# One side bank for the long TensorE tiles, and a new list of VectorE's exp groups, in a fused attention and MLP kernel

## The chip, the core and the metric

The kernel runs on one core of a Trainium2 chip. The metric is the device time of one execution in microseconds, as the median over runs. The profile comes from one execution that the hardware profiler recorded. Its engines are TensorE (PE, with its weight loads as PEld), VectorE (DVE), ScalarE (ACT), GpSimd (POOL) and SyncE (SP), which issues most of the DMAs.

## The reference

The sequence has 2048 rows of 448 columns, in bf16. There are 16 heads of 28 columns, and the inner width of the MLP is 1792.

```python
xn = _layernorm(x, axis=-1)
s = _A_ref(xn, A_wqkv, A_wo)          # attention: softmax(q k^T * 28**-0.5) v, then @ wo
g = _silu(_B_ref(xn, B_w1, B_b1, B_w2, B_b2))   # gelu(xn @ w1 + b1) @ w2 + b2, then silu
return x + s * g
```

## The kernel before

**Blocks and tiles.** The heads are put in four groups `g` of four heads, the rows in four chunks `c` of 512. A block is one pair (g, c), so there are 16 of them, run in the order of `b = 4 g + c`. A block has 64 score tiles of 128 x 512: 16 key tiles `t` for each of four heads `j`. In all there are MTOT = 1024 tiles, numbered by `m`. The last block is cut into three parts of 256, 128 and 128 query columns, so that the end comes in small steps. A score matmul (L1223) uses 32 rows of TensorE's array, and those of different heads run side by side. P*V (L1494) adds 32-column matmuls into one PSUM bank, `acc`; four of them run side by side.

**The banks.** PSUM has eight banks: six of `ring`, and `acc` and `misc`. Units of score tiles alternate between ring banks 0 to 2 (three tiles) and 4 to 5 (two tiles). ScalarE's exp (L1279) reads a whole unit at once and writes bf16 tiles into free places of `P`, `h` or `xnT`. `acc` belongs to P*V once it has begun. Two side banks are left, `misc` and ring bank 3, for everything else: the projections of Q and K (`p_q`, `p_k`, L744), of V (`p_v0`, `p_v1`, L1031), the first MLP matrix (`p_f1`, L1089), the second (`p_f2`, L1158), the output projection (`p_out`, L1591), the sums and reciprocals at a block's end (`p_epi`), and score tiles for VectorE.

**VectorE's groups.** `QUADS` lists groups of four consecutive tiles, `4 q` to `4 q + 3`, whose exp VectorE computes. For each tile a score matmul goes into a side bank (`p_late`), either joined to a unit's score task or by itself, and VectorE evicts it with a scale and an offset into 16-bit integers (`p_apass`, L1382). Five VectorE instructions over 2048 columns (`p_expq`, L1433 to L1440) then make the three summands of the exp, which P*V reads as three tiles in place of one. Each group needs three places of 2048 columns until P*V has read them.

**The order of the work.** The order of instructions is made while the kernel is built. Every piece of work is a Python generator; it yields tasks for an engine, or asks for a bank under a condition. A planner (`run`) keeps an estimated time for each engine and each buffer, and always puts the task that can start first. Among tasks of one engine that can start within EPS = 0.1 us of each other, it goes by priority (scores before most others) and then by the order in which the pieces of work were spawned. The engines then run their fixed lists, each strictly in order, with semaphores between them. The condition with which a projection asks for a bank before the change is this:

```python
bank, tok = yield ("bank", lambda: K.ready(K.b_xnT[c] + [K.b_wqk[1][g]]) and (g == 0 or K.boot()))
```

The bank goes to the piece of work as soon as the inputs are ready and a bank is free, and comes back after VectorE has evicted it. For `p_f2` seven tasks of two matmuls each lie between the two. Fillers (`p_busy`, L905) add zeros to `acc` where the planner sees TensorE too little in use for its clock.

**Stages.** The start (layer norm, transposes, projections of group 0) takes some 20 us. Then the stream of exps runs to the end, with the other work between. Before block 9 is over ScalarE runs the whole GELU at once (L1138), partly from ring banks. F2 and silu's tanh (L1173) follow, then the output projections. Chunks 0 to 2 of the output are added into DRAM by DMAs on GpSimd's queue (L1608), where the input was copied before; the last chunk is added on VectorE and stored by SP. `late_on` is set when the layer norm and the transposes are done, and lets VectorE's groups begin.

Of the kernel before, what the change touches and what calls it, by code (L numbers as in the profile page):

```python
# [18 lines left out]
G = 4  # L19
C = 4  # L20
# [7 lines left out]
MTOT = NBLK * T * 4  # L28

GM = 64 * 9 + 6  # L30
QUADS = (17, 22, 25, 36, 37, 59, 65, 72, 82, 87, 99, 103, 115, 122, 129, 135, 138, 142, 152, 153, 157, 158, 164, 168, 178, 180, 194, 199, 211, 213, 222, 229, 234, 242)
SM_SCALE = DH ** -0.5
LOG2E = 1.4426950408889634
EXP_A3, EXP_A2, EXP_LC = 0.16391228, 0.00783292, 1.1187538523466403
# [5 lines left out]
ND = 9  # L40
# [36 lines left out]
class _Kernel:  # L77
# [132 lines left out]
    def run(self):  # L210
        idle = 0
        while True:
# [25 lines left out]
            self.put(p[3], s)  # L238
            self.advance(p)

    def ready(self, toks, ahead=0.0):
        return all(b.tw is not None and b.tw <= self.now + ahead for b in toks)

# [143 lines left out]
    def schedule(self):  # L387
        K = self
        K.n_f1 = 0
        K.exp_u = -1  # L390
        K.exp_m = -1
        K.late_ready = []
        K.sc_u = -1
        K.pv_m = -1
        K.E_done = -1
        K.norms_done = False
        K.stg_done = 0
        K.qsqs = [0, 1]
        K.qn = [[] for _ in range(G)]
        K.qn_done = 0  # L400
        K.q0_done = 0
        K.f2n = [0] * C
        K.pv_started = False
        K.chunks_done = 0
        K.g_done = [False] * C
        K.on_done = [False] * NBLK
        K.on4 = [False] * 4
        K.ln_done = 0
        K.taken = 0
        K.next_m = 0  # L410
        K.n_late = 0
        K.gu = None
        K.pend = None
        K.units = []
        K.pv_done = [False] * MTOT
        K.late = {4 * q + k for q in QUADS for k in range(4)}
        K.late_left = [sum(1 for q in QUADS if K.sub_of(4 * q) == b) for b in range(NBLK + 3)]
        K.late_on = False
        K.PB, K.PPREV, K.plast = {}, {}, {}
        K.free_u = []  # L420
        K.a_left = {}
        K.ln2e = 0
        K.late_blk = 0
        K.banks += [(K.ring[:, b, :], K.b_ring[b]) for b in (3, 2)]
        K.outs = []
        K.gelu_done = False
        K.dir_n = 0
        K.dir_read = 0
        self.constants()
        self.loads()  # L430
        for c in range(C):
            K.spawn(K.p_ln(c), c)
        K.spawn(K.p_first(), 0)
        K.spawn(K.p_scores(), 0)
        K.spawn(K.p_take(2), 0)
        K.spawn(K.p_exps(), 0)
        K.spawn(K.p_pv(), 0)
        K.spawn(K.p_units(), 0)
        K.spawn(K.p_late(), 0)
        K.spawn(K.p_busy(), 100)  # L440
        o = 1.0

        def nxt():
            nonlocal o
            o += 1.0
            return o
        K.spawn(K.p_norms(), nxt())
        for c in range(1, C):
            K.spawn(K.p_tr(c, 0), nxt())
            K.spawn(K.p_tr(c, 1), nxt())  # L450
            K.spawn(K.p_k(0, c), nxt())
            if c == 1:
                K.spawn(K.p_v0(0), nxt())
            K.spawn(K.p_v0(c), nxt())
        K.spawn(K.p_q(0, 1), nxt())
        for c in (2, 3):
            K.spawn(K.p_q(0, c), nxt())
        for c in range(C):
            K.spawn(K.p_k(1, c), nxt())
        K.spawn(K.p_q(1, 0), nxt())  # L460
        for t in range(T):
            K.spawn(K.p_v1(t), nxt())
        for c in (1, 2, 3):
            K.spawn(K.p_q(1, c), nxt())
        K.spawn(K.p_qn(1), nxt())
        f1 = deque(SBT)
        for c in range(C):
            for _ in range(4):
                K.spawn(K.p_f1(*f1.popleft()), nxt())
            K.spawn(K.p_k(2, c), nxt())  # L470
            K.spawn(K.p_q(2, c), nxt())
        K.spawn(K.p_qn(2), nxt())
        while f1:
            K.spawn(K.p_f1(*f1.popleft()), nxt())
        for c in range(C):
            K.spawn(K.p_k(3, c), nxt())
            K.spawn(K.p_q(3, c), nxt())
        K.spawn(K.p_qn(3), nxt())
        K.spawn(K.p_gelu(), 0)
        K.spawn(K.p_direct(), 0)  # L480
        for c in range(C):
            for t in range(4):
                K.spawn(K.p_f2(c, t), nxt())
            K.spawn(K.p_silu(c), nxt())
        K.o_epi = 0.5
        for c in range(C - 1):
            for t in range(4):
                K.spawn(K.p_out(c, t), nxt())
        for t in range(4):
            K.spawn(K.p_last(t), nxt())  # L490
        K.run()
        for h in K.outs:
            K.wait(SP, h)
# [473 lines left out]

    def p_k(self, g, c):
        K = self
        bank, tok = yield ("bank", lambda: K.ready(K.b_xnT[c] + [K.b_wqk[1][g]]) and (g == 0 or K.boot()))  # L970
        for k in range(2):
            yield K.t_proj(1, g, c, bank, tok, k, 1.5 if g == 0 else 5)
        yield K.t_kev(DVE, g, c, bank, tok, 1 if g == 0 else 2)
        K.banks.append((bank, tok))

    def p_q(self, g, c):
        K = self
        bank, tok = yield ("bank", lambda: K.ready(K.b_xnT[c] + [K.b_wqk[0][g], K.b_colK, K.b_kT[0][3]]) and ((g, c) == (0, 1) or K.boot()))
        for k in range(2):
            yield K.t_proj(0, g, c, bank, tok, k, 1.5 if g == 0 else 5)  # L980
        qb = K.qT[:, g, c * 512:(c + 1) * 512]
        qr = _Buf()
        yield _Task(DVE, lambda eng: eng.tensor_copy(qb, bank), [tok], [qr], 0.7, 0.0, 2)
        K.banks.append((bank, tok))
        yield ("until", lambda: len(K.qsqs) > 0 if g == 0 else (K.qn_done >= g - 1 and (g > 1 or K.q0_done == 3)))
        i = K.qsqs.pop(0) if g == 0 else c
        qs, tq = K.qsq[:, i, :], K.b_qsq[i]
        yield _Task(DVE, lambda eng: eng.tensor_tensor(qs, qb, qb, ALU.mult), [qr], [tq], 0.43, 0.0, 2)
        if g:
            K.qn[g].append(qr)  # L990
            return
        bank2, tok2 = yield ("bank", lambda: K.ready([tq]))
        yield _Task(PE, lambda eng: eng.matmul(bank2, K.bsel[:, :], qs, start=True, stop=True),
                    [tq, K.b_bsel], [tok2], 0.216, 0.17, 1.5 if g == 0 else 4)
        K.qsqs.append(i)
        yield _Task(DVE, lambda eng: eng.scalar_tensor_tensor(qb, bank2, K.colK[:, g:g + 1], qb, op0=ALU.add,
                                                              op1=ALU.add), [tok2, K.b_colK, qr], [qr, K.b_qT[g][c]], 0.75, 0.0, 2)
        K.banks.append((bank2, tok2))
        K.q0_done += 1
# [56 lines left out]
    def p_v1(self, t):  # L1056
        K = self
        rd = [K.b_wv, K.b_wvpad] + K.b_xnT[t // 4]
        bank, tok = yield ("bank", lambda: K.ready(rd + [K.b_vpad]) and K.boot())
        yield _Task(PE, K.t_v([t], 4, 16, bank, tok), rd, [tok], 0.65, 0.17)  # L1060
        yield K.t_vev([t], 4, 16, bank, tok)
        K.banks.append((bank, tok))

    def p_f1(self, c, ft):
        K = self
        bank, tok = yield ("bank", lambda: K.ready(K.b_xnT[c] + [K.b_w1, K.b_w1pad]) and K.stg_done == 2 and K.norms_done)
        for k in range(2):
            yield K.t_f1(c, ft, bank, tok, k)
        wr = [K.b_hf[c][ft]]
        K.hf_free(c, ft)  # L1070
        dst = K.h[:, c, ft * 512:(ft + 1) * 512]
        yield _Task(DVE, lambda eng: eng.tensor_copy(dst, bank), [tok], wr, 0.69, 0.0, 2)
        K.banks.append((bank, tok))
        K.n_f1 += 1
# [73 lines left out]

    def p_f2(self, c, t):
        K = self  # L1150
        bank, tok = yield ("bank", lambda: K.b_h[c].tw is not None and K.ready([K.b_h[c], K.b_w2]) and K.dir_read == ND and (c < 2 or K.g_done[c - 2]))
        hv = K.h[:, c, :].rearrange("p (f n) -> p f n", n=512)
        ps = bank[:, 0:D]
        for q in range(7):
            def f(eng, q=q):
# [3 lines left out]
                                     start=(ft == 0), stop=(ft == FT - 1))  # L1159
                return ins  # L1160
            yield _Task(PE, f, [K.b_w2, K.b_h[c]], [tok], 0.378, 0.17)
        fb = K.fsb[:, c % 2, t, :]
        yield _Task(DVE, lambda eng: eng.tensor_tensor(fb, ps, K.b2b[:, :], ALU.add), [tok, K.b_b2], [K.b_fsb[c % 2]],
                    0.63, 0.0, 2)
# [446 lines left out]
    
    def p_out(self, c, t):
        K = self
        bank, tok = yield ("bank", lambda: K.on_done[(G - 1) * C + c] and K.g_done[c])
        ps = bank[:, 0:D]
        yield K.t_wo(ps, tok, c, t, (0, 1))
        yield K.t_wo(ps, tok, c, t, (2, 3))
        yield from K.t_oev(ps, tok, c, t)
        K.banks.append((bank, tok))

# [62 lines left out]
```

## Time and profile before

| What | us |
|---|---|
| median of 5 runs | 461.03 |
| lowest and highest | 460.93, 461.48 |
| the profiled execution's own time | 460.93 |
| its span, first to last instruction | 459.1 |

In a row of the page's group table, the line, the engine, the operation and the tiles come first, then how many there were, the busy time and the mean duration in ns, then the engine's idle time just before them and what ended it. A row of the waits reads: who waited, for whom, the total in us, how often, and the longest. A row of the timeline begins with the start and the length in us. Durations of neighbours on one engine can overlap, so the time from one start to the next is often shorter than a duration. The row of PEclk gives TensorE's granted clock in tenths, over 40 equal slices of the span.

### The profile page before, as it was taken

What the parts mean: (1) busy time and instruction counts of PE and PEld (TensorE: products, weight loads), DVE (VectorE), ACT (ScalarE), POOL (GpSimd) and SP (SyncE); (2) the same over time, 40 slices, a digit from 0 to 9 for tenths busy, and PEclk for the clock granted to TensorE, in tenths of its full rate; (3) what the DMA queues carried; (4) which work ended last, traced back from release to release, by engine and by line L of the source; (5) the groups of instructions that cost most, each with busy time, mean ns of one, the idle gap of its engine ahead of it and who ended that gap; (6) DMA issues with size and microseconds to landing.
All of it is one profiled execution on the core that took longest, in us unless ns stands there. A gap on an engine that the chain in (4) does not pass through costs nothing.

```text
span 459.1 us, 10615 instructions
## 1 busy us (share of the span) xinstructions
PE 436.2 (95%) x4431; PEld 161.8 (35%) x4431; DVE 372.9 (81%) x584; ACT 446.8 (97%) x408; POOL 41.0 (9%) x85
## 2 busy tenths in 40 slices
PE   6999999999999999999999999999999999989994
PEld 5533333333332323323233333333323333343452
DVE  8956898894897797978989989847778978999964
ACT  6999999999999999999999999999999999999994
POOL 7470000000000000000000000000000100101111
PEclk9999999999999999999999999999999999999998
DMA  8701000000000000000040000000000001300331
GB/s 263 274 2 37 2 1 0 1 1 4 1 1 0 1 2 3 1 2 1 0 143 1 2 0 2 1 1 0 1 1 2 1 0 43 42 1 1 42 43 41
DMA packets 8049, 11.16 MB, mean 24 GB/s; under 512 B 1697, under 2 KB 6993, under 8 KB 7954
## 3 DMA queue, kind: packets, MB, share of 16 engines
q1 hardware_dynamic: 6850, 8.43, 5.9%
q0 software_dynamic: 864, 1.38, 2.5%
q8 instruction: 35, 0.57, 0.5%
q10 hardware_dynamic: 288, 0.69, 0.4%
q14 instruction: 12, 0.10, 0.1%
HBM read 8.61 MB, written 3.21 MB: 26 GB/s over the span
## 4 chain that ended last, share of the span: by engine, by line
PE 42%; ACT 41%; issue 12%; DVE 3%; DMA 1%; POOL 0%; ACTq 0%; DVEq 0%; POOLq 0%
ACT P L1279 20%; PE ring L1223 12%; ACT xnT L1279 10%; ACT h L1279 8%; PE acc L1494 7%; PE ring L1089 5%; PE acc L905 3%; PE misc L1158 2%; PE misc L744 2%; PE misc L1089 2%; PE ring L1158 2%; PE ring L744 2%; PE misc L1223 1%; ACT w L1173 1%; PE ring L1031 1%
## 5 line engine op out<-in xcount | busy, mean ns | idle before, releaser
L1279 ACT ACTIVATE P<-ring 128x1024 bf16<-128x1024 f32 (+1 forms) x188 | 217.5, 1263 | 1.4 <-PE ring L1223 1.0
L1223 PE MATMUL ring<-qT,kT 32*128 32x512 bf16 (+2 forms) x1074 | 145.1, 358 | 11.4 <-ACT P L1279 5.6
L1279 ACT ACTIVATE h<-ring 128x1024 bf16<-128x1024 f32 (+1 forms) x102 | 117.7, 1264 | 0.2
L1223 PEld LDWEIGHTS ring<-qT,kT 32*128 32x128 bf16 x1074 | 37.6, 91 | 134.1 <-ACT P L1279 55.3
L1279 ACT ACTIVATE xnT<-ring 128x1536 bf16<-128x1536 f32 (+1 forms) x72 | 83.4, 1306 | 0.0
L1494 PE MATMUL acc<-P,vaug 128*32 128x512 bf16 (+2 forms) x524 | 49.2, 358 | 0.0
L1089 PE MATMUL ring<-xnT,w 128*128 128x512 bf16 x156 | 41.4, 382 | 1.1 <-ACT h L1138 0.9
L1564 POOL CAST rhi<-rc 128x16 bf16<-128x16 f32 x15 | 6.0, 401 | 365.2 <-DVE rc L1562 297.0
L905 PE MATMUL acc<-ident,zero 128*128 128x128 bf16 x393 | 34.3, 221 | 0.0
L1223 PE MATMUL misc<-qT,kT 32*128 32x512 bf16 (+1 forms) x78 | 29.2, 376 | 0.0
L905 PEld LDWEIGHTS acc<-ident,zero 128*128 128x128 bf16 x393 | 22.3, 98 | 18.8 <-issue 18.2
L1494 PE MATMUL acc<-h,vaug 128*32 128x512 bf16 x248 | 27.6, 384 | 0.0
L1158 PE MATMUL misc<-w,h 128*128 128x448 bf16 x112 | 27.3, 356 | 0.0
L1158 PE MATMUL ring<-w,h 128*128 128x448 bf16 x112 | 27.2, 355 | 0.0
L1382 DVE TENSOR_SCALAR x_sb<-misc 128x512 uint16<-128x512 f32 x31 | 21.3, 687 | 6.2 <-PE misc L1223 5.9
L1089 PE MATMUL misc<-xnT,w 128*128 128x512 bf16 x68 | 19.5, 383 | 0.5 <-DVE qT L1581 0.5
L1552 DVE CAST E_sb<-acc 128x512 bf16<-128x512 f32 x15 | 10.4, 690 | 11.7 <-PE acc L1494 11.7
L1494 PE MATMUL acc<-xnT,vaug 128*32 128x512 bf16 (+2 forms) x240 | 18.7, 330 | 0.9 <-ACT P L1279 0.7
L1089 PEld LDWEIGHTS ring<-xnT,w 128*128 128x128 bf16 x156 | 12.1, 97 | 20.0 <-issue 7.2
L1494 PEld LDWEIGHTS acc<-P,vaug 128*32 128x32 bf16 x524 | 11.8, 94 | 15.0 <-issue 11.8
L1382 DVE TENSOR_SCALAR kT<-ring 128x512 uint16<-128x512 f32 x19 | 13.1, 688 | 4.3 <-PE ring L1223 3.4
L1138 ACT ACTIVATE h<-h 128x2048 bf16<-128x2048 bf16 (+2 forms) x8 | 16.2, 2031 | 0.0
(269 smaller groups left out, 662.5 us busy)
## 6 DMA issues: line engine op xcount, KB each, us to landing
w<-in_B_w_dram SPq DMA_DIRECT2D x1, 1568.0 KB, 7.7
w<-in_B_w_dram SPq DMA_DIRECT2D x1, 1344.0 KB, 8.5
out_dram<-in_A_x_dram SPq DMA_DIRECT2D x3, 448.0 KB, 11.3
out_dram<-h POOLq DMA_DIRECT2D x6, 224.0 KB, 3.9
x_sb<-in_A_x_dram SPq DMA_DIRECT2D x2, 448.0 KB, 5.7
h<-in_A_wqkv_dram SPq DMA_DIRECT2D x3, 168.0 KB, 5.1
x_sb<-in_A_x_dram ACTq DMA_DIRECT2D x1, 448.0 KB, 4.5
h<-in_A_x_dram SPq DMA_DIRECT2D x1, 448.0 KB, 4.2
```

The costliest lines, as they stand in the source:

```text
L744: ins = eng.matmul(bank, w[:, kt, g * 128:(g + 1) * 128], K.xnT[:, kt, c * 512:(c + 1) * 512], start=(kt == 0), stop=(kt == KT - 1))
L905: ins = eng.matmul(K.acc[:, 0:128], K.zero[:, :], K.ident[:, :], start=False, stop=True, skip_group_check=True)
L1031: ins = eng.matmul(bank[:, off:off + nh * 32], K.xnT[:, kt, t * 128:(t + 1) * 128], ap, start=(kt == 0), stop=(kt == KT - 1), skip_group_c ...
L1089: ins = eng.matmul(bank, K.w1[:, kt, ft * 128:(ft + 1) * 128], K.xnT[:, kt, c * 512:(c + 1) * 512], start=(kt == 0), stop=(kt == KT - 1))
L1138: yield _Task(ACT, lambda eng, dst=dst, src=src: eng.activation(dst, src, ACTF.Gelu_apprx_tanh), rd, wr, 0.4267 * n + (0.1 if pc else 0.06 ...
L1158: ins = eng.matmul(ps, hv[:, ft, t * 128:(t + 1) * 128], K.w2[:, ft, :], start=(ft == 0), stop=(ft == FT - 1))
L1223: return eng.matmul(dst, K.kT[32 * j:32 * j + 32, g, t * 128:(t + 1) * 128], K.qT[32 * j:32 * j + 32, g, c * 512 + q0:c * 512 + q0 + nq], ...
L1279: return eng.activation(reg[:, i0:i0 + n, :], K.ring[:, b0:b0 + n, :], ACTF.Exp, scale=SM_SCALE)
L1382: yield _Task(DVE, lambda eng: eng.tensor_scalar(K.unit[u][:, 512 * k:512 * k + 512].bitcast(dt.uint16), bank, SM_SCALE * LOG2E * 128.0, ( ...
L1494: return eng.matmul(K.acc[32 * j:32 * j + 32, q0:q0 + nq], K.vaug[:, t, 4 * g + j, :], ap[:, col:col + nq], tile_position=(0, 32 * j), sta ...
L1552: yield _Task(DVE, lambda eng: eng.tensor_copy(E, K.acc[:, :]), [K.b_acc], [tE], 0.7, 0.0, 0)
L1564: yield _Task(POOL, lambda eng: eng.tensor_copy(K.rhi[:, :], K.rc[:, :]), [K.b_rc], [K.b_rhl], 1.1, 0.0, 1)
```

## The change

There are two edits. The list `QUADS` goes from 34 groups to 35, and only ten groups stand in both lists. By block, the eleventh (counted from one) goes from two groups to three, the fourteenth from three to two and the fifteenth from two to three; the other blocks keep their number, with most groups in other places. The second edit counts the pieces of work that hold a side bank and still have matmuls to issue. While the count is not zero, no other piece of these kinds gets a bank: `p_k`, `p_q`, `p_v1`, `p_f1`, `p_f2` and `p_out`. The count goes down after the last matmul is put, before VectorE's eviction. Before `late_on` the gate is open.

```diff
-QUADS = (17, 22, 25, 36, 37, 59, 65, 72, 82, 87, 99, 103, 115, 122, 129, 135, 138, 142, 152, 153, 157, 158, 164, 168, 178, 180, 194, 199, 211, 213, 222, 229, 234, 242)
+QUADS = (17, 18, 25, 37, 41, 58, 68, 70, 81, 90, 97, 98, 117, 124, 131, 135, 140, 142, 146, 154, 157, 159, 161, 162, 165, 183, 185, 197, 200, 210, 211, 225, 229, 234, 242)
...
+    def pe_free(self):
+        return self.pe_wait == 0 or not self.late_on
...
+        K.pe_wait = 0
...
     def p_f2(self, c, t):
         K = self
-        bank, tok = yield ("bank", lambda: K.b_h[c].tw is not None and K.ready([K.b_h[c], K.b_w2]) and K.dir_read == ND and (c < 2 or K.g_done[c - 2]))
+        bank, tok = yield ("bank", lambda: K.pe_free() and K.b_h[c].tw is not None and K.ready([K.b_h[c], K.b_w2]) and K.dir_read == ND and (c < 2 or K.g_done[c - 2]))
+        K.pe_wait += 1
...
             yield _Task(PE, f, [K.b_w2, K.b_h[c]], [tok], 0.378, 0.17)
+        K.pe_wait -= 1
...
     def p_out(self, c, t):
         K = self
-        bank, tok = yield ("bank", lambda: K.on_done[(G - 1) * C + c] and K.g_done[c])
+        bank, tok = yield ("bank", lambda: K.pe_free() and K.on_done[(G - 1) * C + c] and K.g_done[c])
+        K.pe_wait += 1
         ps = bank[:, 0:D]
         yield K.t_wo(ps, tok, c, t, (0, 1))
         yield K.t_wo(ps, tok, c, t, (2, 3))
+        K.pe_wait -= 1
```

`p_k`, `p_q`, `p_v1` and `p_f1` get the same three lines around their matmuls.

More of the change, by code (lines that the diff above doesn't have):

```diff
@@ L969, in p_k @@
         K = self
-        bank, tok = yield ("bank", lambda: K.ready(K.b_xnT[c] + [K.b_wqk[1][g]]) and (g == 0 or K.boot()))
+        bank, tok = yield ("bank", lambda: K.pe_free() and K.ready(K.b_xnT[c] + [K.b_wqk[1][g]]) and (g == 0 or K.boot()))
+        K.pe_wait += 1
         for k in range(2):
             yield K.t_proj(1, g, c, bank, tok, k, 1.5 if g == 0 else 5)
+        K.pe_wait -= 1
         yield K.t_kev(DVE, g, c, bank, tok, 1 if g == 0 else 2)
@@ L977, in p_q @@
         K = self
-        bank, tok = yield ("bank", lambda: K.ready(K.b_xnT[c] + [K.b_wqk[0][g], K.b_colK, K.b_kT[0][3]]) and ((g, c) == (0, 1) or K.boot()))
+        bank, tok = yield ("bank", lambda: K.pe_free() and K.ready(K.b_xnT[c] + [K.b_wqk[0][g], K.b_colK, K.b_kT[0][3]]) and ((g, c) == (0, 1) or K.boot()))
+        K.pe_wait += 1
         for k in range(2):
             yield K.t_proj(0, g, c, bank, tok, k, 1.5 if g == 0 else 5)
+        K.pe_wait -= 1
         qb = K.qT[:, g, c * 512:(c + 1) * 512]
@@ L1058, in p_v1 @@
         rd = [K.b_wv, K.b_wvpad] + K.b_xnT[t // 4]
-        bank, tok = yield ("bank", lambda: K.ready(rd + [K.b_vpad]) and K.boot())
+        bank, tok = yield ("bank", lambda: K.pe_free() and K.ready(rd + [K.b_vpad]) and K.boot())
+        K.pe_wait += 1
         yield _Task(PE, K.t_v([t], 4, 16, bank, tok), rd, [tok], 0.65, 0.17)
+        K.pe_wait -= 1
         yield K.t_vev([t], 4, 16, bank, tok)
@@ L1065, in p_f1 @@
         K = self
-        bank, tok = yield ("bank", lambda: K.ready(K.b_xnT[c] + [K.b_w1, K.b_w1pad]) and K.stg_done == 2 and K.norms_done)
+        bank, tok = yield ("bank", lambda: K.pe_free() and K.ready(K.b_xnT[c] + [K.b_w1, K.b_w1pad]) and K.stg_done == 2 and K.norms_done)
+        K.pe_wait += 1
         for k in range(2):
             yield K.t_f1(c, ft, bank, tok, k)
+        K.pe_wait -= 1
         wr = [K.b_hf[c][ft]]
@@ L1150, in p_f2 @@
         K = self
-        bank, tok = yield ("bank", lambda: K.b_h[c].tw is not None and K.ready([K.b_h[c], K.b_w2]) and K.dir_read == ND and (c < 2 or K.g_done[c - 2]))
+        bank, tok = yield ("bank", lambda: K.pe_free() and K.b_h[c].tw is not None and K.ready([K.b_h[c], K.b_w2]) and K.dir_read == ND and (c < 2 or K.g_done[c - 2]))
+        K.pe_wait += 1
         hv = K.h[:, c, :].rearrange("p (f n) -> p f n", n=512)
@@ L1161, in p_f2 @@
             yield _Task(PE, f, [K.b_w2, K.b_h[c]], [tok], 0.378, 0.17)
+        K.pe_wait -= 1
         fb = K.fsb[:, c % 2, t, :]
@@ L1613, in p_out @@
         K = self
-        bank, tok = yield ("bank", lambda: K.on_done[(G - 1) * C + c] and K.g_done[c])
+        bank, tok = yield ("bank", lambda: K.pe_free() and K.on_done[(G - 1) * C + c] and K.g_done[c])
+        K.pe_wait += 1
         ps = bank[:, 0:D]
@@ L1617, in p_out @@
         yield K.t_wo(ps, tok, c, t, (2, 3))
+        K.pe_wait -= 1
         yield from K.t_oev(ps, tok, c, t)
```

## The prediction

> **What bounds the kernel now.** I read the page first (busy shares and the clock row), then the waits by engine, then the groups by form, then ScalarE's timeline, and last the timeline of the end.
>
> ```profile
> PE 436.2 (95%) x4431; PEld 161.8 (35%) x4431; DVE 372.9 (81%) x584; ACT 446.8 (97%) x408; POOL 41.0 (9%) x85
> ...
> PEclk9999999999999999999999999999999999999998
> ```
>
> TensorE (PE) and ScalarE (ACT) both look full, so the shares alone do not tell which one leads. The waits do.
>
> ```profile
> PEld ring L1223 <- ACT P L1279: 55.3, 135, 0.8
> PEld ring L1223 <- ACT h L1279: 33.2, 78, 0.6
> ...
> PEld ring L1223 <- ACT xnT L1279: 19.5, 49, 0.7
> ```
>
> ```profile
> ACT P L674 <- DMA x_sb<-in_A_x_dram: 2.3, 1, 2.3
> ACT P L1279 <- PE ring L1223: 1.0, 3, 0.5
> ```
>
> The score matmuls (L1223) wait 108 us in 262 places for ScalarE's exp (L1279) to give a bank back; ScalarE's recorded waits for scores are 1.0 us. Also 393 of TensorE's matmuls, 34.3 us of busy time, are fillers (L905) without work in them. So ScalarE leads, and a time for the change is a time for ScalarE: how many exps it runs, and how often one starts late. The exps by form:
>
> ```profile
> L1279 ACT ACTIVATE P<-ring 128x1536 bf16<-128x1536 f32 x85 | 127.6, 1501 | 0.5 <-PE ring L1223 0.2
> L1279 ACT ACTIVATE P<-ring 128x1024 bf16<-128x1024 f32 x102 | 106.5, 1070 | 0.9 <-PE ring L1223 0.8
> L1279 ACT ACTIVATE h<-ring 128x1536 bf16<-128x1536 f32 x44 | 66.4, 1508 | 0.2
> L1279 ACT ACTIVATE h<-ring 128x1024 bf16<-128x1024 f32 x58 | 61.7, 1079 | 0.0
> L1279 ACT ACTIVATE xnT<-ring 128x1536 bf16<-128x1536 f32 x36 | 54.6, 1515 | 0.0
> L1279 ACT ACTIVATE xnT<-ring 128x1024 bf16<-128x1024 f32 x36 | 39.5, 1096 | 0.0
> ...
> L1279 ACT ACTIVATE P<-ring 128x512 bf16<-128x512 f32 x1 | 0.6, 639 | 0.0
> ```
>
> There are 165 exps over three tiles, 196 over two and one over a single tile: 888 tiles. Their durations overlap, so the price of one is its pitch, from start to start:
>
> ```profile
> 306.27 1.16 ACT L1279 ACTIVATE P<-ring 128x1024 bf16<-128x1024 f32 x1
> 307.17 7.03 ACT L1279 ACTIVATE xnT<-ring 128x1536 bf16<-128x1536 f32 x6
> ```
>
> An exp of two tiles is followed after 0.90 us. Over all starts in the trace the common pitch is 0.904 us for two tiles, 1.330 us for three and 0.478 us for the single one. At these pitches the stream costs 196 x 0.904 + 165 x 1.330 + 0.478 = 397.1 us. The real starts add 8.3 us to that, 6.7 us of it in 41 exps that start more than 0.06 us late. The page hides these, because a late start first eats the overlap of the durations (1.070 - 0.904 = 0.17 us) before it shows as idle time. In most of the 41 TensorE ran a projection, F1 or F2 task, or a P*V task, when the bank came back.
>
> **The change, part by part.**
>
> The list: 35 groups of four tiles leave ScalarE where 34 did, so 884 tiles stay. In the changed instruction order there are 164 three-tile and 196 two-tile exps, and no single one: 196 x 0.904 + 164 x 1.330 = 395.3 us. ScalarE saves 1.330 + 0.478 = 1.81 us. It is on the path at full value, since ScalarE's stream is almost without a pause from the first exp at 13.94 us to the last at 451.82 us.
>
> VectorE (DVE) takes the group: four evictions (L1382) at 0.69 us and the five steps of its exp (L1433 to L1440): three of 0.69 us and two of 1.22 us. That is 2.75 + 4.5 = 7.3 us, and nine instructions. VectorE is idle for 459.1 - 372.9 = 86 us; its share goes from 81% to 83%. Where the time lies matters more. Counting instructions in program order by the durations of their rows, the 15 exps that follow the 230th had 9.9 us of VectorE work beside 18.6 us of ScalarE, and get 17.0 us. Other stretches of 15 exps already stand at 0.95 to 1.04 in the present order, and in the new one the fullest (exps 110 to 125) stands at 1.05. I cost it at nothing; the cover is VectorE's idle time within each block, and if it is gone the rival below holds.
>
> TensorE: scores stay at 960 matmuls. A VectorE tile needs three P*V matmuls in place of one: 4 x 2 = 8 more, and 8 of them take 0.45 us, four running side by side. The fillers go from 393 to 429, 36 x 0.056 = 2.0 us, put where TensorE would pause. Both lie in TensorE's waits for ScalarE (108 us). Cost: nothing by themselves.
>
> The gate (`pe_free`, `pe_wait`): while one projection, V, F1, F2 or output tile has matmuls left, no second one may take a side bank. Such tiles finish one after the other in the present order too, so no matmul is lost by this; what it changes is that the second bank stays free for score tiles of VectorE's groups. VectorE waits for those scores now, for example
>
> ```profile
> DVE x_sb L1382 <- PE misc L1223: 5.9, 11, 1.8
> ...
> DVE kT L1382 <- PE ring L1223: 3.4, 7, 1.0
> ```
>
> This gives VectorE room rather than time. The price is that F2 tiles finish some exps later: the last one's eviction stands behind exp 304 where it stood behind 297, and the tanh over its chunk moves with it. The output projections of the last chunk but one move from before VectorE's copy of the last block's first half to after it. Both are far from what needs them, except at the end.
>
> The queues: GpSimd (POOL) and SP keep their order of instructions. SP's twelve norm-row DMAs stay with their blocks; the first four come after exp 88 instead of 86, their issues take about 2.3 us, and the scores that read them start at exp 99, some 9 us on. GpSimd's last two accumulating output DMAs (issue 0.87 us, landing 3.9 us) move from 439.5 and 441.9 us to roughly 446 and 450 us, ahead of two multiplications that now start at 453.00 us. That leaves about 3 us; without it, each issue would add its 0.87 us to the end.
>
> The end: from the last exp's end (452.46 us) to the span's end there are 6.7 us: P*V, copy, sum, reciprocal, two products, output product, add, DMA. The same chain stands in the new order. No change.
>
> Late starts are the unknown term. Counting the TensorE work between each unit's scores and the next (row times: scores 0.32 us, F1 or projection pair 0.43 us, F2 pair 0.38 us, eight P*V matmuls 0.45 us), 65 gaps outside the start hold over 0.1 us more than the exp that must cover them; in the new order 66. Without the GELU stretch the sum of the excess goes from 16.2 to 18.6 us. At the present rate (8.3 us late for 16.2 us of excess) this is +1.2 us; but the count is coarse and names only part of the places where exps are late, so the other end is -1.0 us (the freed bank spreads score tiles more evenly). One place I can name: the P*V task for the first half of the last block now waits for the last group's final product, with 1.22 + 0.26 + 0.69 + 1.22 = 3.4 us of VectorE work behind its copy of the accumulator, while TensorE has about 3.1 us to do. Some 0.3 us may show there. I take +0.5 us in all, nearer the count than zero, and keep -1.0 and +2.0 for the range.
>
> [...]
>
> Sum: -1.8 + 0.5 = -1.3 us. The profiled execution took 460.93 us with a span of 459.1 (1.8 us around it), 0.1 us under the median of 461.03. So 461.03 - 1.3 = 459.7 us.
>
> **The rivals.** About 0.2%, 0.9 us, is what a measurement of this kernel can tell from no change.
>
> *The gain is eaten by late starts.* Denser P*V and score tasks make exps late by as much as the shorter stream saves, +1.0 to +2.5 us. For it: the excess count. Against it: the number of overfull gaps hardly moves, 65 to 66. Time: 460.2 to 461.9 us, about 461.0.
>
> *Slower: TensorE stands behind VectorE.* TensorE issues in order. At a block's end its P*V task waits for VectorE's group or copy, and the next scores stand behind that task. ScalarE has at most one unit in hand; a two-tile exp leaves about 0.904 - 0.32 - 0.24 = 0.34 us of slack. If VectorE is one 1.22 us product late, 1.22 - 0.34 = 0.9 us reaches ScalarE. Places: the blocks that now hold three groups (the eleventh and the fifteenth), exps 110 to 125, and the end. It decides from about 2.3 us, three such ends; with four, 461.03 - 1.8 + 3.6 = 462.8 us. For it: those stretches are full. Against it: TensorE's waits for VectorE's copy are only 2.1 us in 5 places now, and no copy of the accumulator stands directly behind a product in either order.
>
> *The gate does nothing, or more than I think.* If it is inert, only the list counts: -1.8 us, 459.2 us. If it also evens out the scores, late starts fall by 1.0 us: 461.03 - 2.8 = 458.2 us.
>
> **How the numbers follow.** Forecast with late starts between 0 and +0.9 us (459.2 to 460.1): 0.43. The better case (below 459.2): 0.18. Gain eaten: 0.21, nearly all within 0.9 us of the median. TensorE behind VectorE, over 462: 0.18. Faster by over 0.2% means below 460.1: 0.43 + 0.18 = 0.61, less a little for its upper edge: 0.60. Within: 0.21. Slower: 0.19. The range leaves the best tail and half of the slow case outside: 458.5 to 462.0 us. The likeliest case's own range is 458.5 to 460.1 us.
>
> **What would show each step.** ScalarE's groups: 164 exps of 1536 and 196 of 1024 columns at the same pitch, and no form of 512. VectorE's busy time up by about 7 us, near 380. Late starts summed over the exps: near 8.8 us; at 10 or more the gain is eaten, at 7 the gate helps TensorE. If TensorE stands behind VectorE, the waits list P*V (acc) behind VectorE's products or copies with several us, and ScalarE's idle time rises above its present 12.3 us. The PEclk row should stay at 9. The prediction is wrong in kind if ScalarE's stream is no longer closed, or if the end after the last exp is over 7.5 us.

## The result: 459.90 us against 461.02, and the profile after

| | before | after |
|---|---|---|
| median of the runs | 461.02 us (37 runs) | 459.90 us (19 runs) |
| ratio to before | | 0.9976, 95% interval 0.997 to 0.9982 |
| the profiled execution, time and span | 460.93, 459.1 us | 459.70, 457.9 us |

The kernel is 1.1 us faster, 0.24%, and the interval lies on one side of 1. Medians are over all runs, and ratios leave out disturbed runs, of which the experiments had three (754.8, 1328.5 and 481.5 us). The page of the changed kernel answers the page shown before the change:

```profile
PE 436.5 (95%) x4475; PEld 163.5 (36%) x4475; DVE 381.0 (83%) x593; ACT 445.2 (97%) x406; POOL 45.0 (10%) x85
...
PEclk9999999999999999999999999999999999999999
```

VectorE gained 8.1 us of work and nine instructions, ScalarE lost two instructions and 1.6 us, and TensorE's granted clock stayed up (its mean is 0.999, and 0.996 in the kernel before). The score matmuls are now L1237, the exps L1293, P*V L1508. The waits keep their direction: score matmuls wait for ScalarE's exps, and ScalarE waits for scores very little.

```profile
PEld ring L1237 <- ACT P L1293: 52.5, 130, 0.7
...
PEld ring L1237 <- ACT h L1293: 30.8, 72, 0.8
```

```profile
ACT P L678 <- DMA x_sb<-in_A_x_dram: 2.3, 1, 2.3
ACT P L1293 <- PE ring L1237: 1.3, 4, 0.5
```

ScalarE's groups by form show which exps went:

```profile
L1293 ACT ACTIVATE P<-ring 128x1536 bf16<-128x1536 f32 x85 | 127.4, 1499 | 0.4 <-PE ring L1237 0.3
L1293 ACT ACTIVATE P<-ring 128x1024 bf16<-128x1024 f32 x101 | 105.5, 1071 | 1.1 <-PE ring L1237 1.0
L1293 ACT ACTIVATE h<-ring 128x1536 bf16<-128x1536 f32 x44 | 65.6, 1490 | 0.2
L1293 ACT ACTIVATE h<-ring 128x1024 bf16<-128x1024 f32 x59 | 61.7, 1057 | 0.2 <-PE ring L1237 0.2
L1293 ACT ACTIVATE xnT<-ring 128x1536 bf16<-128x1536 f32 x35 | 52.3, 1494 | 0.1
L1293 ACT ACTIVATE xnT<-ring 128x1024 bf16<-128x1024 f32 x36 | 38.7, 1076 | 0.0
```

There are 164 three-tile exps for 165, 196 two-tile exps as before, and the form of 512 columns is gone. The whole span can be divided up by ScalarE's starts; the parts add up to it by construction. "Pitch" is the number of exps times their common distances (1.330, 0.904 and 0.478 us), the last one included. "Late" is what the real starts add to it. "Other" is GELU, tanh and the table loads between the first and the last exp. "End" is what lies behind the last exp's pitch.

| us | first exp | pitch | late | other | end | span |
|---|---|---|---|---|---|---|
| before | 12.59 | 397.11 | 8.30 | 34.29 | 6.83 | 459.1 |
| after | 12.60 | 395.30 | 8.96 | 34.29 | 6.75 | 457.9 |

The difference is -1.80 us of pitch, +0.66 us of late starts and -0.09 us at the end, together the -1.2 us between the spans.

### The profile page after: what moved, and what is told of

It reads as the page before. It is cut to its first block, busy times and chain, and to the rows that moved or that the text cites. A ratio compares the mean times of both kernels' runs of the same rounds, so it can differ in the third digit from the quotient of the medians.

```text
span 457.9 us, 10703 instructions
## 1 busy us (share of the span) xinstructions
PE 436.5 (95%) x4475; PEld 163.5 (36%) x4475; DVE 381.0 (83%) x593; ACT 445.2 (97%) x406; POOL 45.0 (10%) x85
## 4 chain that ended last, share of the span: by engine, by line
PE 52%; ACT 32%; issue 11%; DVE 3%; DMA 1%; POOL 0%; ACTq 0%; DVEq 0%; POOLq 0%
PE ring L1237 15%; ACT P L1293 15%; PE acc L1508 9%; ACT h L1293 7%; ACT xnT L1293 7%; PE ring L1101 6%; PE ring L1171 4%; PE acc L909 3%; PE ring L748 3%; PE misc L1101 2%; PE misc L748 2%; PE misc L1039 1%; ACT h L1150 1%; PE ring L1039 1%; PE misc L1171 1%
## 5 line engine op out<-in xcount | busy, mean ns | idle before, releaser
L1293 ACT ACTIVATE P<-ring 128x1024 bf16<-128x1024 f32 (+1 forms) x186 | 214.8, 1267 | 1.4 <-PE ring L1237 1.3
L1237 PE MATMUL ring<-qT,kT 32*128 32x512 bf16 (+2 forms) x1075 | 145.4, 358 | 10.9 <-ACT P L1293 3.9
L1293 ACT ACTIVATE h<-ring 128x1024 bf16<-128x1024 f32 (+1 forms) x103 | 118.4, 1242 | 0.4 <-PE ring L1237 0.2
L1237 PEld LDWEIGHTS ring<-qT,kT 32*128 32x128 bf16 x1075 | 37.5, 91 | 133.0 <-ACT P L1293 52.5
L1293 ACT ACTIVATE xnT<-ring 128x1536 bf16<-128x1536 f32 (+1 forms) x71 | 82.3, 1282 | 0.1
L1508 PE MATMUL acc<-P,vaug 128*32 128x512 bf16 (+2 forms) x526 | 48.4, 356 | 0.0
L1101 PE MATMUL ring<-xnT,w 128*128 128x512 bf16 x164 | 43.1, 382 | 0.2 <-ACT h L1150 0.2
L1171 PE MATMUL ring<-w,h 128*128 128x448 bf16 x154 | 37.4, 355 | 0.0
L909 PEld LDWEIGHTS acc<-ident,zero 128*128 128x128 bf16 x429 | 24.3, 98 | 15.4 <-issue 14.5
L1237 PE MATMUL misc<-qT,kT 32*128 32x512 bf16 (+1 forms) x77 | 28.7, 377 | 0.0
L1508 PE MATMUL acc<-h,vaug 128*32 128x512 bf16 x250 | 28.0, 384 | 0.0
L1396 DVE TENSOR_SCALAR x_sb<-ring 128x512 uint16<-128x512 f32 x26 | 17.8, 686 | 2.8 <-PE ring L1237 2.6
L1508 PE MATMUL acc<-xnT,vaug 128*32 128x512 bf16 (+2 forms) x232 | 18.1, 333 | 0.0
L1508 PEld LDWEIGHTS acc<-P,vaug 128*32 128x32 bf16 x526 | 12.0, 94 | 16.0 <-issue 13.4
L1566 DVE CAST E_sb<-acc 128x512 bf16<-128x512 f32 x15 | 10.4, 691 | 8.3 <-PE acc L1508 8.3
L1171 PEld LDWEIGHTS ring<-w,h 128*128 128x128 bf16 x154 | 11.2, 97 | 17.1 <-issue 10.2
L1101 PE MATMUL misc<-xnT,w 128*128 128x512 bf16 x60 | 17.2, 383 | 0.0
L1396 DVE TENSOR_SCALAR kT<-misc 128x512 uint16<-128x512 f32 x20 | 13.8, 688 | 4.2 <-PE misc L1237 4.2
L1396 DVE TENSOR_SCALAR x_sb<-misc 128x512 uint16<-128x512 f32 x22 | 15.1, 685 | 2.4 <-PE misc L1237 2.1
```

Of the source, the lines that this page charges most:

```text
L909: ins = eng.matmul(K.acc[:, 0:128], K.zero[:, :], K.ident[:, :], start=False, stop=True, skip_group_check=True)
L1101: ins = eng.matmul(bank, K.w1[:, kt, ft * 128:(ft + 1) * 128], K.xnT[:, kt, c * 512:(c + 1) * 512], start=(kt == 0), stop=(kt == KT - 1))
L1171: ins = eng.matmul(ps, hv[:, ft, t * 128:(t + 1) * 128], K.w2[:, ft, :], start=(ft == 0), stop=(ft == FT - 1))
L1237: return eng.matmul(dst, K.kT[32 * j:32 * j + 32, g, t * 128:(t + 1) * 128], K.qT[32 * j:32 * j + 32, g, c * 512 + q0:c * 512 + q0 + nq], ...
L1293: return eng.activation(reg[:, i0:i0 + n, :], K.ring[:, b0:b0 + n, :], ACTF.Exp, scale=SM_SCALE)
L1396: yield _Task(DVE, lambda eng: eng.tensor_scalar(K.unit[u][:, 512 * k:512 * k + 512].bitcast(dt.uint16), bank, SM_SCALE * LOG2E * 128.0, ( ...
```

## The experiments

All times are medians. Every kernel was compared with the kernel before on the same chip, whose median was 460.96 to 461.01 us. The columns of the table above, for all kernels with a usable profile; the number of groups stands in brackets where it is needed, and the span is these columns and the first exp's start, which lies between 12.56 and 13.19 us:

| us | time | pitch | late | other | end |
|---|---|---|---|---|---|
| gate, list of before (34) | 468.96 | 397.11 | 14.02 | 36.53 | 6.60 |
| no gate, new list (35) | 480.75 | 395.30 | 26.28 | 37.00 | 7.77 |
| gate, new list less 161 (34) | 463.41 | 397.11 | 9.73 | 34.28 | 7.23 |
| gate for F2 only, new list | 470.03 | 395.30 | 16.21 | 36.99 | 7.04 |
| gate, new list, 16 places in P | 475.32 | 395.30 | 21.62 | 37.09 | 6.73 |
| no gate, new list, P first | 474.24 | 395.30 | 20.03 | 36.87 | 7.52 |
| gate, new list, P first | 462.10 | 395.30 | 10.18 | 34.62 | 7.53 |
| no gate, 35 groups fitted | 463.26 | 395.30 | 11.32 | 34.29 | 7.55 |
| gate, 36 groups fitted | 458.65 | 393.55 | 8.81 | 34.30 | 7.50 |
| gate, 34 groups fitted | 462.36 | 397.11 | 8.38 | 35.31 | 6.82 |
| gate, new list, 124 to 127 | 469.97 | 395.30 | 16.21 | 37.09 | 6.74 |

**The gate alone.** The changed kernel with `QUADS` of before.

```diff
-QUADS = (17, 18, 25, 37, 41, ...)
+QUADS = (17, 22, 25, 36, 37, ...)   # the 34 groups of the kernel before
```

> The gate alone, with the 34 groups of the kernel before. Theory (ScalarE's number of exps at their pitch sets the time, late starts are the rest): the floor of the exps stays at 397.1 us, late starts stay within 1 us of the 8.3 us of before, so 460.0 to 462.0 us, likeliest 461.2. Rival A (the gate itself makes the time by freeing a side bank): late starts fall below 7.3 us and the time below 460.0. Rival B (the gate costs, since TensorE is held back): over 462.0 us with late starts above 9.5 us.

It took 468.96 us, ratio 1.0171 (1.0158 to 1.0184), well outside what the theory allowed. Late starts went to 14.0 us, 3.0 us of them in one exp, and "other" grew by 2.2 us because GELU waited for F1. So "the number of exps sets the time, and the gate costs nothing by itself" falls. The signs of rival B came (over 462.0 us, late starts above 9.5 us); how much of it is the gate's own price is told by the fitted list further down. The one exp says more. In ScalarE's timeline of this run the bracket at the end of a row is the idle time before it and what ended that:

```profile
75.09 4.68 ACT L1293 ACTIVATE h<-ring 128x1536 bf16<-128x1536 f32 x4
82.56 1.45 ACT L1293 ACTIVATE P<-ring 128x1536 bf16<-128x1536 f32 x1 [2.78 <-PE acc L1508]
```

ScalarE did not wait for scores. It waited 2.78 us for P*V (L1508). In this kernel an exp needs free places for its tiles, and a place becomes free when P*V has read it.

**The list without the gate.**

```diff
     def pe_free(self):
-        return self.pe_wait == 0 or not self.late_on
+        return True
```

> The list of 35 groups with the gate always open. Theory that the list alone carries the gain: floor 395.3 us, late starts 8 to 9.5 us, 459.2 to 460.3 us, the same as the changed kernel. Rival (the gate is what makes room for the 35th group; this list was laid out for it): VectorE gets its score tiles later, TensorE stands more often behind it, late starts above 10 us, 460.8 us or more.

It took 480.75 us, ratio 1.0427 (1.0413 to 1.0440). The theory that the list alone carries the gain is wrong by 20 us; the rival that the list needs the gate's order has the right signs. VectorE does get its score tiles later, as it said: VectorE's evictions (L1396) wait 37.1 us for scores here, over all tiles, and 19.8 us in the changed kernel. The largest row of these waits, here first and then in the changed kernel:

```profile
DVE kT L1396 <- PE misc L1237: 11.0, 11, 4.7
```

```profile
DVE kT L1396 <- PE misc L1237: 4.8, 12, 0.8
```

ScalarE's waits in this run, and VectorE's, TensorE's and ScalarE's rows at the largest stop:

```profile
ACT P L1293 <- PE acc L1508: 14.7, 4, 5.4
ACT h L1150 <- PE ring L1101: 2.5, 2, 1.6
```

```profile
344.67 1.23 DVE L1454 TENSOR_TENSOR kT<-kT,x_sb 128x2048 bf16<-128x2048 f16 x1
...
347.35 0.69 DVE L1566 CAST E_sb<-acc 128x512 bf16<-128x512 f32 x1 [0.32 <-PE acc L1508]
```

```profile
346.04 0.62 PE L1508 MATMUL acc<-P,vaug 128*32 128x512 bf16 x8
346.47 0.40 PE L1508 MATMUL acc<-x_sb,vaug 128*32 128x512 bf16 x4
346.68 0.62 PE L1508 MATMUL acc<-kT,vaug 128*32 128x512 bf16 x8
```

```profile
341.08 1.02 ACT L1293 ACTIVATE P<-ring 128x1024 bf16<-128x1024 f32 x1
347.48 2.37 ACT L1293 ACTIVATE P<-ring 128x1536 bf16<-128x1536 f32 x2 [5.39 <-PE acc L1508]
```

In order: VectorE ends the block's last product at 345.90 us. The block's last P*V task follows at 346.04 us and reads eight tiles in P and the late group. Then comes VectorE's copy of the accumulator (L1566), and ScalarE goes on at 347.48 us after 5.39 us of idle time. The planner issues a block's last P*V only when all the block's groups are done (`late_left` in `p_pv`). Every stop above 1 us in this run, five of them, has the same signature: an exp that starts 0.1 us after such a copy has begun.

**One group less.** The changed kernel without group 161.

```diff
-QUADS = (..., 157, 159, 161, 162, 165, ...)
+QUADS = (..., 157, 159, 162, 165, ...)
```

> The changed kernel without group 161 (the eleventh block goes back from three groups to two), so 34 groups with the gate. Theory: four tiles go back to ScalarE, +1.7 us of floor (4 x 0.4267 us, and one exp more at its fixed part), late starts as in the changed kernel within 0.7 us: 461.0 to 462.3 us. Rival (the 35th group is paid back by late starts, so that it brings little): late starts fall by 1 us or more and the time stays under 460.7 us.

It took 463.41 us, 3.5 us over the changed kernel and 1.1 us more than expected. The pitch part is +1.8 us, about as expected; late starts add 0.8 us and the end 0.5 us. So the group is not paid back, the rival falls, but taking one out of a fitted list costs more than its exps.

**The gate for F2 only.** The five other kinds of tile still count, but do not wait; one of the five edits is shown.

```diff
     def p_f1(self, c, ft):
-        bank, tok = yield ("bank", lambda: K.pe_free() and K.ready(K.b_xnT[c] + [K.b_w1, K.b_w1pad]) and ...)
+        bank, tok = yield ("bank", lambda: K.ready(K.b_xnT[c] + [K.b_w1, K.b_w1pad]) and ...)
```

> The changed kernel with the gate asked only by F2's tiles (the others still count, but do not wait). The list has 35 groups. If the gate matters only where F2's seven tasks hold a bank, the time is that of the changed kernel, 459.6 to 460.2 us. If it matters for projections and F1 too, late starts before exp 210 grow and it lies nearer to the list without a gate. If the list alone matters, no difference among the three beyond 0.6 us.

It took 470.03 us, about halfway between the changed kernel and the list without a gate. Before GELU its stops are those of the list without a gate (2.5 us at 82 us, 1.1 at 111, 3.7 at 167). After GELU, where the ungated list stood for 5.5 and 3.6 us, no exp is more than 0.6 us late. So the gate acts on each stage's own tiles: on the projections and F1 as well as on F2.

**Without the late group.** The ungated list less 165, the last group of the eleventh block.

```diff
-QUADS = (..., 161, 162, 165, 183, ...)      # no gate
+QUADS = (..., 161, 162, 183, ...)
```

> The list without a gate, less group 165, the last of the three groups of the eleventh block. In the list without a gate ScalarE stood 5.5 us at 347 us, until the block's last P*V had run, 1.6 us after the final product of this very group. Theory (a block's last P*V waits for its last group, holds eight tiles in P meanwhile, and ScalarE stops when P has no free place): that stop goes, +1.8 us for four more tiles on ScalarE, the other stops stay within some us: 475 to 478.5 us, no stop above 2 us between 330 and 360 us. Rival (side banks or TensorE's order make the stop, not this group): a stop of over 4 us stays there, 480.5 us or more.

It took 477.52 us, as the theory had it: 3.2 us less, although four tiles went back to ScalarE. Its profile cannot be used, so that the stop itself is gone was not seen.

**Two places less in P.**

```diff
-NP = 18
+NP = 16
```

> The changed kernel with 16 places in P for exp tiles instead of 18; nothing else. If free places in P are the room that covers a late group, two tiles of room less, 2 x 0.43 = 0.85 us, reach ScalarE at each block end that had no spare room: late starts go up by 1 to 8 us, with stops that end just after a block's last P*V; 461 to 468 us. Rival (P has room to spare in this list, and TensorE's tasks alone make exps late): within 0.7 us of 459.9.

It took 475.32 us (its runs lie between 472.98 and 481.54), in the theory's direction but far above its range. ScalarE's waits, a row of TensorE's timeline, and the clock from the page:

```profile
ACT P L1293 <- PE acc L1508: 9.2, 3, 4.7
ACT P L1293 <- PE ring L1237: 4.3, 6, 1.4
```

```profile
30.62 0.40 PE L728 MATMUL misc<-ident,h 128*128 128x128 bf16 x4 [1.47 <-DVE h L710]
```

```profile
PEclk9988999999999999999999999999999999999999
```

Two block ends stop for 4.9 and 3.3 us; that is the theory's part, and the rival, that P has room to spare, falls. Five exps in the first 40 us are 5.6 us late together, which I had not thought of. One of them, 1.4 us late, waits for P*V. The other four wait for scores: TensorE had paused for 1.47 us behind the layer norm on VectorE (L710), and after that its granted clock was 0.51 from 32 to 36 us and 0.63 from 36 to 40 us. The run with a mean granted clock of 0.999 took 472.98 us; the two at 0.992, one of them this profile, took 475.14 and 475.51. So 2.2 to 2.5 us of the loss go with the lower clock. The size was misjudged because I counted two tiles of room, and neither the new order that they bring nor the clock.

**P first at the block's end.** If a group is late, the eight tiles in P go to P*V without it.

```diff
+            early = end and len(mine()) < K.late_left[b]
+            if early:
+                yield from self.pv_task(q, [], ms)
+                for m in ms:
+                    K.pv_done[m] = True
+                K.pv_m = ms[-1]
             while end and len(mine()) < K.late_left[b]:
...
-            yield from self.pv_task(q, late, ms)
+            if late or not early:
+                yield from self.pv_task(q, late, [] if early else ms)
```

> The list without a gate, but at a block's end the eight tiles that lie in P go to P*V at once, and only the group that is late comes after. Theory of the P places: eight places come free some us earlier, worth up to 8 x 0.43 = 3.4 us of exps per stop, so the stops of 2.5, 3.7, 5.5 and 3.6 us go to below 2.2 us each: 466 to 473 us. Rival (the stop comes from the accumulator: the next block's P*V cannot begin before VectorE has copied it): the stops stay, 478 us or more.

> The changed kernel with the same edit at the block's end. It has no stop above 0.5 us, so by the theory there is nothing to gain at block ends; the task is cut in two, which lets scores go between. 459.3 to 460.6 us. If the order shifts so that groups come later at other blocks, stops of over 1 us appear and it is 461 us or more.

Without the gate it took 474.24 us, 6.5 us less than the same list without the edit, but above the range. The stops at 82, 111, 167 and 404 us are gone. The one at 347 us is not: it now ends at 348 us and is longer, 6.5 us, and a new one of 5.3 us ends at 244 us. Both end 1.7 to 1.8 us after the copy of the accumulator (L1573 in this kernel) has begun. Freed places help, and then the next block's tiles fill P, because their P*V cannot begin before that copy: ScalarE's two waits for P*V in this run are 11.2 us, the longest 6.3. So both the theory and its rival hold a part. With the gate it took 462.10 us, 2.2 us over the changed kernel, with no stop above 0.6 us: late starts +1.2 us, the end +0.8 us, and GELU's stage +0.3 us. I had expected no change or stops; the loss came in small pieces of another order.

**One group moved.** The direct test on the changed kernel itself.

```diff
-QUADS = (..., 117, 124, 131, ...)
+QUADS = (..., 117, 127, 131, ...)
```

> The changed kernel with one group moved: 124 becomes 127, the last four tiles of the eighth block. Same counts, same gate; the order up to the seventh block is unchanged. Theory (a block's last P*V waits for its last group, and ScalarE stops when P is full): a stop of 1 to 5 us at the end of the eighth block, about 225 to 245 us into the span, that ends just after that block's last P*V; 461 to 466 us. Rival (late groups cost nothing, P's places and the next block's scores cover them): no stop over 0.6 us there, within 0.7 us of 459.9.

It took 469.97 us. The stop stands where it was expected, and the time is 4 us above the range, since later blocks and GELU's stage were also set back (2.5 us at 369 us, "other" +2.8 us). ScalarE's and VectorE's timelines at the end of the eighth block:

```profile
237.53 1.59 ACT L1293 ACTIVATE h<-ring 128x1536 bf16<-128x1536 f32 x1
242.80 1.02 ACT L1293 ACTIVATE h<-ring 128x1024 bf16<-128x1024 f32 x1 [3.68 <-PE acc L1508]
244.84 1.45 ACT L1293 ACTIVATE P<-ring 128x1536 bf16<-128x1536 f32 x1 [1.02 <-PE acc L1508]
```

```profile
240.23 1.22 DVE L1454 TENSOR_TENSOR x_sb<-x_sb,w 128x2048 bf16<-128x2048 f16 x1
```

And TensorE's:

```profile
239.18 0.39 PE L1237 MATMUL ring<-qT,kT 32*128 32x512 bf16 x4 [0.32 <-ACT h L1293]
239.50 2.18 PE L909 MATMUL acc<-ident,zero 128*128 128x128 bf16 x36
241.62 0.40 PE L1508 MATMUL acc<-h,vaug 128*32 128x512 bf16 x4
```

The scores for the next exp are there at 239.6 us, so they are not what is missing. Nor are they stuck behind P*V in TensorE's order: TensorE runs 36 fillers until VectorE's product, which ends at 241.45 us, lets P*V begin. What is missing is a free place for the exp's tiles. The counts of exps and of groups are those of the changed kernel; one group, three places later in the list, costs 10 us.

**Lists fitted to the order.** For the next three, the planner laid out some thousand lists for the given gate and number of groups, and the list that it held to be the shortest was run.

```diff
# no gate, 35 groups
+QUADS = (17, 22, 30, 33, 36, 57, 67, 75, 83, 88, 100, 105, 116, 121, 130, 135, 141, 143, 146, 150, 157, 159, 161, 165, 179, 186, 193, 195, 209, 211, 215, 225, 229, 232, 244)
# gate, 36 groups
+QUADS = (17, 22, 34, 40, 49, 56, 67, 77, 83, 94, 97, 101, 117, 126, 130, 131, 132, 143, 145, 149, 150, 157, 162, 167, 171, 177, 184, 193, 199, 205, 209, 216, 225, 230, 231, 243)
# gate, 34 groups
+QUADS = (23, 36, 44, 54, 62, 70, 73, 87, 94, 101, 108, 114, 116, 131, 132, 135, 140, 142, 154, 155, 158, 162, 166, 172, 182, 185, 197, 203, 211, 218, 223, 229, 234, 242)
```

> 35 groups without the gate, with a list that was fitted to the gateless order (the planner laid out some thousand lists, and the one that it thought the shortest is run; nothing of its estimate is used here). Theory (a list has to fit the order, and 35 groups fit without the gate too once fitted): floor 395.3 us, late starts 9 to 11 us, 459.8 to 461.8 us. Rival (the gate is needed for 35 groups, VectorE gets its scores too late without it): stops of over 1 us at block ends and late starts above 12 us, 462.5 us or more.

> The gate with 36 groups and a list fitted to it in the same manner. Theory: the floor falls by four more tiles, 1.7 to 1.8 us, and late starts stay between 8.5 and 10.5 us if VectorE's 7.3 us more still end before each block does: 457.9 to 459.8 us, under the changed kernel. Rival (VectorE is full with 35): late starts above 11 us, 460.5 us or more.

> The gate with 34 groups and a list fitted to it. The floor is that of the kernel before. If the gate changes late starts by little once the list fits, 460.4 to 462.0 us, within 1 us of the kernel before and far under the 468.96 us of the gate with the list unfitted. If the gate holds TensorE back whatever the list, 464 us or more.

The gate with 34 fitted groups took 462.36 us (ratio 1.0028, 1.0017 to 1.0039): 6.6 us under the unfitted list with the gate, so most of that loss was the misfit. But it lies 0.4 us above the range that I gave, and has no gain over the kernel before: late starts are 8.4 us, but the first exp comes 0.6 us later and GELU's stage is 1.0 us longer. Without the gate, 35 fitted groups took 463.26 us (1.0037 to 1.0062). That is 17 us under the new list without the gate, with no stop above 0.9 us, but 3.4 us over the changed kernel: late starts 11.3 us against 9.0, and the end 0.8 us longer. The time is the rival's (462.5 us or more); its signs, stops of over 1 us and late starts above 12 us, are not there. 35 groups do fit without the gate, at a price that the fit did not remove; whether a better list exists there stays open.

The gate with 36 fitted groups took **458.65 us**, ratio 0.9955 (0.9943 to 0.9968), under both kernels and within the theory's range. Its slowest run, 459.43 us, is faster than the fastest of the changed kernel, 459.70. Its page:

```profile
PE 434.2 (95%) x4471; PEld 164.7 (36%) x4471; DVE 386.4 (85%) x602; ACT 443.1 (97%) x405; POOL 42.3 (9%) x85
```

VectorE takes one group more than in the changed kernel, and late starts stay at 8.8 us. Against the kernel before, pitch is 3.6 us shorter, late starts 0.5 us and the end 0.7 us longer, which is the 2.4 us between the spans.

## Why the prediction was right, and where its reasons were not

The sum was -1.8 + 0.5 = -1.3 us and 459.7 us; it measured -1.1 us and 459.9.

- *The pitch.* Predicted -1.81 us, measured -1.80. The forms came out as counted. (The stream's first exp is at 12.59 us; the 13.94 us that I read is the second's.)
- *Late starts.* Predicted 8.8 us, measured 8.96. The +0.66 us lies between my two estimates, the count of overfull gaps (65 to 66, so about nothing) and the scaled sum (+1.2 us), about midway. My +0.5 us was a choice between them, and that it came so close is in part luck. In number the late exps hardly changed: 41 were over 0.06 us late before, 40 after.
- *The place that I named at the end.* It was 0.49 us late where I said 0.3, for another reason. The product of the last group is ready long before P*V asks for it, by these rows of VectorE's, TensorE's and ScalarE's timelines:

```profile
434.84 1.23 DVE L1454 TENSOR_TENSOR x_sb<-x_sb,kT 128x2048 bf16<-128x2048 f16 x1
```

```profile
437.17 0.16 PEld L1508 LDWEIGHTS acc<-xnT,vaug 128*32 128x32 bf16 x8
...
438.42 0.68 PE L1237 MATMUL ring<-qT,kT 32*128 32x128 bf16 x20
...
438.86 1.02 ACT L1293 ACTIVATE P<-ring 128x1024 bf16<-128x1024 f32 x1 [0.21 <-PE ring L1237]
```

  The product ends at 436.07 us and P*V begins at 437.17. What made the exp late is one task of 40 P*V matmuls, from there to 438.41 us, that stood before the scores.
- *The end and the queues.* The end was costed at nothing and came out 0.09 us shorter. GpSimd's last two output DMAs went out at 442.20 and 448.96 us (I said 446 and 450), 2.9 us before its multiplications at 451.82.
- *The clock.* Fillers went to 429 as counted, and the granted clock was 1.00 from 20 to 440 us, as in the kernel before. The longest pause of TensorE in the changed kernel in that stretch is 0.52 us. With 16 places in P, the granted clock was 0.51 from 32 to 36 us, behind a pause of 1.47 us, and the two runs at a mean clock of 0.992 took 2.2 and 2.5 us longer than the one at 0.999. That the pause made the clock fall was not shown: no run varied the pause alone.
- *VectorE costs nothing, its cover being idle time within each block.* The work was 8.1 us where I said 7.3, and it did cost nothing with this list; but idle time is the wrong cover. With the same work, one group moved three places costs 10 us (124 to 127). The cover is that each block's last product ends before P fills. I had not looked at that, so here the right number rests on the list having been fitted.
- *"If the gate is inert, only the list counts: 459.2 us".* Wrong. The list with the gate off takes 480.75 us, and the gate with the old list 468.96 us. Neither half has a price of its own; each list fits one order.
- *The slow rival.* I had TensorE standing in order behind VectorE, with scores behind it. Where the slow case does occur, TensorE runs fillers or other work, and ScalarE stops for a free place. My price of 0.9 us at a block's end was too low: in the list without the gate the five stops are 1.1 to 5.5 us. In the changed kernel it does not occur at all, as its ScalarE waits show.

The better case, late starts 1.0 us lower, did not come; nor did it with 36 groups. What the gate brings, by the lists that were run, grows with the number of groups: at 34 it costs 1.4 us against the kernel before, at 35 it saves 3.4 us against the fitted list without it, and 36 take off a further 1.3 us. That it makes room for groups is the likely reading, but not shown: 36 groups without it were not run, and each case has one fitted list.

## What to carry to other kernels

Read the leading engine by its starts, not by its busy share: number times common pitch, plus the late starts, plus the rest, makes up the span (here 395.30, 8.96 and 53.64 us of 457.9) and shows where one percent can still lie. Where a planner lays out the order, a rule of the planner and a list tuned under it are one change; undoing either half measures the misfit, not its worth, so refit before judging. Work moved to an idle engine costs nothing only as long as its last piece ends before whoever waits for it runs out of buffers (with the same work on VectorE, one group moved by three places cost 10 us here); look at the deadline, not at the engine's idle total.

## What the runs showed that I had not expected

The size of the answer to a small change of order: 10 us from moving one of 35 groups by three places, 15 us from two places of P, 2.2 to 2.5 us of it in the runs whose mean granted clock was 0.992 in place of 0.999. The pitch of an exp did not move in any of these kernels: 0.904 us for two tiles and 1.330 us for three, in the kernel that took 480.75 us as in the one that took 458.65 us.
